# The upper halves of the first three units' values, issued by ScalarE instead of SyncE

## The chip, the cores and the metric

The kernel runs on one core of a Trainium2 chip. A core has TensorE (PE: matmuls, and the loads of their weights, PEld), VectorE (DVE), ScalarE (ACT), GpSimd (POOL) and SyncE (SP), each with its own instruction stream, and 16 DMA engines. SyncE here only issues transfers; ScalarE computes and can issue transfers too. The metric is the time of one execution on the device in microseconds, lower is better.

## The reference

Chunked attention with memory rows feeds a gated feed-forward layer with spatial mixing. Batch 4, 8 heads, 768 positions, head size 64; chunks of 32 positions.

```python
for c in range(nc):                       # 24 chunks
    l_start, r_end = max(0, c_start - 16), min(S, c_end + 8)
    k_full = concat([mem_k, k[:, :, l_start:r_end]])      # 8 memory rows first
    v_full = concat([mem_v, v[:, :, l_start:r_end]])
    a = softmax(scale * q_c @ k_full.T)
    out[:, :, c_start:c_end] = a @ v_full
x = out as (batch, seq, 512)
h = relu(x @ w_in)                        # 512 x 1024
u, v = h[..., :512], h[..., 512:]
v_n = (v - mean) / sqrt(var + 1e-6)
v_s = einsum('ts,bsd->btd', w_spatial, v_n) + b_spatial
y = (u * v_s) @ w_out
```

## The kernel before

The attention is cut into 24 units of four chunks (six units for each batch). For a unit `i` the steps are: ScalarE copies its keys into a padded tile (`prep`, L375, `kmain`); TensorE multiplies 64 small tiles of queries and keys into `sx` (L388, `sx<-kmain,q`, "scores"); VectorE takes the row maximum and subtracts it (L441, L445); ScalarE's exponential (L450) makes `p`; VectorE sums and inverts (L455, L456, L458, `den` and `rec`); TensorE transposes `p` (L472, `pt`), ScalarE copies it (L475, `pT`); TensorE multiplies with the values (L388, `sx<-vmain,pT`, "product with values"); VectorE normalises (L424, `xs`); TensorE transposes `xs` (L487, `xt`); ScalarE's cast (L492) and VectorE's subtraction (L496) split the result into a high and a low part of `x`. `sx` has one buffer: the product of unit i - 1 shares a buffer with the scores of unit i, and the next pair waits until both have been read.

The feed-forward product runs in three matmuls for each piece (L525 to L527, `f`: high by high, low by high, high by low). Its weights `w_in` come in eight pieces of 512 columns by 128 rows, four for the second half of the columns (needed first) and four for the first half. Each piece is loaded into one of four `big` buffers and prepared in steps on three engines: ScalarE scales it twice (L825, L830), VectorE does a shift pair (L834, L835), GpSimd adds (L840), ScalarE casts to the high part (L854), and VectorE or GpSimd subtracts for the low part (L858, `win_l`).

Values: `load_v(i)` fetches a unit's values into its third of `vmain`. The lower half of the partitions (r = 0) takes the even heads and the upper half (r = 1) the odd ones, each in two transfers, of 32 rows (128 KB) and of 24 rows (96 KB); the eight rows between hold the memory values. All of these stand on SyncE, in the order in which the code lists them with the queries, keys and weights (`line` ties each to the one ahead).

No engine's order is written out by hand. Every step is an `op` with an engine, an estimated time, what it reads and writes and a rank; `Plan.order` runs a list schedule with these estimates, and all instructions are emitted in the order of its start times. A transfer's estimated end is its size times `drag` by a rate, added to the end of the one ahead. So a change of one load's engine, of its `drag` or of what it stands behind (`after`) moves rows on all engines. On the chip each engine works through its rows strictly in that order. Transfers of all engines take one of eight completion counters in turn, and one is issued only when the transfer eight before it has landed; `held_by` adds a limit on the bytes under way.

## Time and profile before

| | |
|---|---|
| median of 3 runs | 380.65 us (380.58 to 384.18) |
| the profiled execution | 378.39 us, span 376.2 us |
| TensorE busy | 355.6 us (95%) |
| VectorE busy | 275.0 us (73%) |
| ScalarE busy | 188.8 us (50%) |
| GpSimd busy | 139.8 us (37%) |
| share of TensorE in the chain that ended last | 91% |

Times in the rows are microseconds from the start of the span. A row of the timeline has its start, its duration, the engine, the line, the operation, the tile written and the tile read, the shapes, and in brackets how long the engine was idle before it and what ended that. SPq and ACTq are the issues of transfers by SyncE and ScalarE. A row of the waits has total time, number of times and the longest. A row of stretches has the stretch, its length, busy time (and number of instructions) of PE, PEld, DVE, ACT and POOL, the clock granted to TensorE (1.00 is full), the mean busy share of the DMA engines and their GB/s.

### The profile page before, as it was taken

The numbers are of one execution on the slowest core, as the hardware profiler recorded it, in microseconds if no ns is written. First come the engines' busy times: TensorE is split into PE (matmuls) and PEld (weight loads), VectorE is DVE, ScalarE is ACT, GpSimd is POOL, SyncE is SP. The second block draws the span as 40 slices with busy tenths as digits, with TensorE's granted clock in tenths as the row PEclk, the third lists the DMA queues.
The fourth block names the chain that finished last, engine by engine and source line by source line (L and its number), as shares of the span: only waits on it lengthen the run. The fifth ranks groups of instructions, "written<-read, shape, count | busy, mean of one in ns | idle before, by whom it ended". The sixth has DMA issues, their size and how long they took to land.

```text
span 376.2 us, 11734 instructions
## 1 busy us (share of the span) xinstructions
PE 355.6 (95%) x4964; PEld 327.8 (87%) x4964; DVE 275.0 (73%) x470; ACT 188.8 (50%) x336; POOL 139.8 (37%) x143
## 2 busy tenths in 40 slices
PE   1569899999999999999999999999999999999996
PEld 1357698898988988989889899999999999999996
DVE  3887875757767667775498589787858795896694
ACT  3757544554654456354473366327533742553371
POOL 5444652383484088510033195251026002203410
PEclk9969999999999999999999999999999999999999
DMA  8998888888786783865832649204720582140014
GB/s 230 290 233 228 186 250 232 230 234 250 218 237 192 251 232 92 264 212 181 233 142 92 216 142 319 101 0 167 250 89 0 170 257 80 61 144 8 2 44 167
DMA packets 47368, 65.12 MB, mean 173 GB/s; under 512 B 4434, under 2 KB 38866, under 8 KB 47316
## 3 DMA queue, kind: packets, MB, share of 16 engines
q1 hardware_dynamic: 46900, 64.25, 56.4%
q8 instruction: 39, 0.64, 0.7%
q10 hardware_dynamic: 416, 0.13, 0.1%
q14 instruction: 13, 0.11, 0.1%
HBM read 45.49 MB, written 18.87 MB: 171 GB/s over the span
## 4 chain that ended last, share of the span: by engine, by line
PE 91%; DVE 4%; ACT 2%; DMA 1%; issue 1%; SPq 0%; ACTq 0%; DVEq 0%
PE y L686 22%; PE f L686 17%; PE f L525 13%; PE f L526 12%; PE f L527 12%; PE sx L388 10%; PE xt L487 3%; PE pt L472 3%; DMA k<-in_k_dram 1%; DVE st L835 1%; DVE st L834 1%; DVE mx L441 1%; DVE p L445 0%; PE y L680 0%; PE f L680 0%
## 5 line engine op out<-in xcount | busy, mean ns | idle before, releaser
L742 POOL TENSOR_TENSOR ug<-st,ug 128x384 f32<-128x384 f32 x24 | 33.1, 1392 | 97.7 <-DVE st L734 97.7
L686 PE MATMUL y<-wsp,op 128*128 128x384 f32 x288 | 52.6, 336 | 0.0
L686 PEld LDWEIGHTS y<-wsp,op 128*128 128x128 f32 x288 | 50.1, 188 | 0.0
L525 PE MATMUL f<-x,win_h 128*128 128x384 f32 x128 | 46.3, 362 | 0.0
L527 PE MATMUL f<-x,win_h 128*128 128x384 f32 x128 | 43.1, 337 | 0.0
L526 PE MATMUL f<-x,win_l 128*128 128x384 f32 x128 | 43.0, 336 | 0.0
L525 PE MATMUL f<-win_h,x 128*128 128x512 f32 x96 | 41.7, 435 | 0.0
L686 PE MATMUL f<-wsp,op 128*128 128x384 f32 x216 | 40.1, 336 | 0.0
L526 PE MATMUL f<-win_h,x 128*128 128x512 f32 x96 | 38.6, 402 | 1.5 <-DVE x L496 1.5
L664 DVE TENSOR_TENSOR op<-sm,op 128x768 fp32r<-128x768 f32 x32 | 33.4, 1050 | 7.2 <-ACT op L661 6.6
L527 PE MATMUL f<-win_l,x 128*128 128x512 f32 x96 | 38.4, 400 | 0.0
L686 PEld LDWEIGHTS f<-wsp,op 128*128 128x128 f32 x216 | 37.6, 188 | 0.0
L686 PE MATMUL y<-wout,op 128*128 128x256 f32 x288 | 35.7, 280 | 0.0
L424 DVE TENSOR_TENSOR xs<-sx,rec 128x512 f32<-128x512 f32 x24 | 16.5, 689 | 25.8 <-PE sx L388 25.6
L686 PEld LDWEIGHTS y<-wout,op 128*128 128x128 f32 x288 | 34.8, 188 | 0.1
L661 ACT CAST op<-sm 128x768 fp32r<-128x768 f32 x32 | 26.3, 838 | 15.5 <-DVE sm L647 7.7
L571 POOL TENSOR_TENSOR rstd<-ve,mhalf 128x1 f32<-128x1 f32 x24 | 14.6, 610 | 52.2 <-DVE ve L567 51.8
L388 PEld LDWEIGHTS sx<-kmain,q 64*32 64x32 f32 x1536 | 17.5, 110 | 17.1 <-POOL vmain L370 9.5
L388 PE MATMUL sx<-kmain,q 64*32 64x64 f32 x1536 | 21.5, 235 | 10.6 <-ACT kmain L375 8.4
L596 ACT ACTIVATE uo<-f 128x384 f32<-128x384 f32 x32 | 15.6, 491 | 24.5 <-PE f L527 23.0
L370 POOL COPY vmain<-memv 8x1024 f32<-8x1024 f32 x22 | 23.5, 1075 | 10.2 <-PE sx L388 8.5
L686 PE MATMUL f<-wout,op 128*128 128x256 f32 x216 | 27.1, 280 | 0.0
(92 smaller groups left out, 732.8 us busy)
## 6 DMA issues: line engine op xcount, KB each, us to landing
vmain<-in_v_dram SPq DMA_DIRECT2D x48, 128.0 KB
vn_far<-st SPq DMA_DIRECT2D x24, 256.0 KB
u_far<-uo SPq DMA_DIRECT2D x32, 192.0 KB
vr<-vn_far SPq DMA_DIRECT2D x8, 768.0 KB
ug<-u_far SPq DMA_DIRECT2D x16, 384.0 KB
q<-in_q_dram SPq DMA_DIRECT2D x11, 512.0 KB
out_dram<-ot SPq DMA_DIRECT2D x36, 128.0 KB
vmain<-in_v_dram SPq DMA_DIRECT2D x47, 96.0 KB
```

Source lines behind the costliest of these rows:

```text
L370: {"DVE": nc.vector, "POOL": nc.gpsimd}[eng].tensor_copy(to, of)
L388: nc.tensor.matmul(o, w_, m, start=True, stop=True, skip_group_check=True)
L424: nc.vector.tensor_tensor(xs.rearrange("p t r d -> p r t d"), t_["sx", i][:, :, 1], rec.rearrange("p t r -> p r t").unsqueeze(3).broadcast ...
L525: nc.tensor.matmul(o, lh, rh, start=(j == 0), stop=False)
L526: nc.tensor.matmul(o, ll, rh, start=False, stop=False)
L527: nc.tensor.matmul(o, lh, rl, start=False, stop=(j == len(pairs) - 1))
L571: nc.gpsimd.tensor_tensor(a, t_["ve", i], mhalf, op=ALU.pow)
L596: op("ACT", act(HT), lambda: nc.scalar.activation(alloc("uo", i, [P, HT], F32), t_["f", n], AF.Relu), r=[("f", n)], w=[("uo", i)], rank=rank)
L661: nc.scalar.copy(half(0), of())
L664: nc.vector.tensor_tensor(half(1), of(), half(0).bitcast(F32), op=ALU.subtract)
L686: nc.tensor.matmul(o, x, y, start=first and m == 1 and not (seed and bank != "x"), stop=m == 3 * chunks, skip_group_check=True)
L742: nc.gpsimd.tensor_tensor(g, t_[st(x)], g, op=ALU.mult)
```

## The change

For units 0, 1 and 2, the two transfers of the upper half of the partitions no longer stand in SyncE's line. They are issued by ScalarE, behind the start of its copy of the same unit's keys (`prep`). The estimate's factor `drag` is 1.2 instead of 1.5 for all transfers of these units' values. From unit 3 on, `load_v` is as it was.

```diff
-    def load_v(i, seq=True, second="SP"):
+    def load_v(i, heads=(0, 1), eng="SP", drag=1.5, after=None):
+
         b, c0 = i // UB, (i % UB) * UC
         n = UC
-        for r in range(2):
+        for r in heads:
...
-                load(dst, src_, w=[("vm", i, r, s)], rank=10.0 * i, slow=1.2, us=0.38, seq=seq, drag=1.5,
-                     eng=second if r else "SP")
+                load(dst, src_, w=[("vm", i, r, s)], rank=10.0 * i, slow=1.2, us=0.38, seq=eng == "SP", drag=drag, eng=eng, after=after)
...
         if i < NU:
             prep(i, rank)
+            if i < 3:
+                load_v(i, (1,), "ACT", 1.2, len(plan.ops) - 1)
         burst(i, rank, split)
...
-    load_v(0)
+    load_v(0, (0,), drag=1.2)
...
-    load_v(1)
+    load_v(1, (0,), drag=1.2)
...
-    load_v(2)
+    load_v(2, (0,), drag=1.2)
```

`load` takes the new argument `after` and hands it to `op`, for loads that are not in a line. Below L505 the changed kernel's line numbers are higher by two.

VectorE's rows from the second shift pair to the first `xs`, before. The numbers tell buffers apart: `st_264`, `st_281`, `st_289` and `st_307` are the first four pieces of `w_in`, `p_287` belongs to unit 1, and `xs_364` is the first normalised result.

```order
L858 TENSOR_TENSOR win_l_110<-st_264,win_h_109 128x512
L834 TENSOR_SCALAR st_289<-st_289 128x512
L835 SCALAR_TENSOR_TENSOR st_289<-big_170,st_289 128x512
L834 TENSOR_SCALAR st_307<-st_307 128x512
L835 SCALAR_TENSOR_TENSOR st_307<-big_172,st_307 128x512
L858 TENSOR_TENSOR win_l_110<-st_281,win_h_109 128x512
L424 TENSOR_TENSOR xs_364<-sx_230,rec_269 128x2x4x64
L455 TENSOR_REDUCE den_366<-p_287 128x8
```

The same place in the changed kernel, where the fourth piece is `st_306` and the first `xs` is `xs_372`:

```order
L860 TENSOR_TENSOR win_l_110<-st_264,win_h_109 128x512
L836 TENSOR_SCALAR st_289<-st_289 128x512
L837 SCALAR_TENSOR_TENSOR st_289<-big_170,st_289 128x512
L860 TENSOR_TENSOR win_l_110<-st_281,win_h_109 128x512
L455 TENSOR_REDUCE den_321<-p_287 128x8
L456 TENSOR_TENSOR den_321<-den_321,eps_104 128x8
L458 RECIPROCAL rec_324<-den_321 128x8
L860 TENSOR_TENSOR win_l_110<-st_289,win_h_109 128x512
L836 TENSOR_SCALAR st_306<-st_306 128x512
L837 SCALAR_TENSOR_TENSOR st_306<-big_172,st_306 128x512
L424 TENSOR_TENSOR xs_372<-sx_230,rec_269 128x2x4x64
```

The sum and reciprocal of unit 1 and one more subtraction for `win_l` have moved ahead of the first `xs`.

ScalarE's rows at the same place of the program, from the last scaling of the fourth piece to the cast of unit 0's result, before:

```order
L830 ACTIVATE big_172<-big_172 128x512
L450 ACTIVATE p_287<-p_287 128x512
L854 CAST win_h_109<-st_281 128x512
L475 COPY pT_362<-pt_318 128x512
L854 CAST win_h_109<-st_289 128x512
L492 CAST x_380<-xt_371 128x4x128
L375 COPY kmain0_144<-k_224 128x20x32
L854 CAST win_h_109<-st_307 128x512
L375 COPY kmain1_145<-k_224 128x20x32
```

And in the changed kernel:

```order
L257 DMA vmain_143<-in_v_dram 32x4x256
L856 CAST win_h_109<-st_281 128x512
L257 DMA vmain_143<-in_v_dram 24x4x256
L450 ACTIVATE p_287<-p_287 128x512
L856 CAST win_h_109<-st_289 128x512
L475 COPY pT_367<-pt_326 128x512
L375 COPY kmain0_144<-k_224 128x20x32
L257 DMA vmain_143<-in_v_dram 32x4x256
L257 DMA vmain_143<-in_v_dram 24x4x256
L375 COPY kmain1_145<-k_224 128x20x32
L856 CAST win_h_109<-st_306 128x512
L492 CAST x_423<-xt_413 128x4x128
```

The exponential of unit 1 stands behind the cast of the second piece, the copies of the keys of units 2 and 3 stand ahead of the fourth piece's cast and of the cast of unit 0's result, and four of the six new issues are seen here (the first two stand between the copies of the keys of units 0 and 1). A little later the scaling of the sixth piece (L827, `big_311`) stands ahead of the exponential of unit 2.

TensorE, from the warming matmuls (L540, L542 in the changed kernel) to the first matmul of the dense stream, before:

```order
L540 MATMUL f_299<-win_h_109 128x512 x4
L472 MATMUL pt_318<-ident_102,p_287 128x128 x4
L388 MATMUL sx_230<-vmain_143,pT_279 32x64 x32
L487 MATMUL xt_371<-ident_102,xs_364 128x128 x4
L388 MATMUL sx_389<-kmain0_144,q_182 32x64 x32
L525 MATMUL f_427<-win_h_109,x_380 128x512
```

And in the changed kernel:

```order
L542 MATMUL f_299<-win_h_109 128x512 x4
L472 MATMUL pt_326<-ident_102,p_287 128x128 x4
L388 MATMUL sx_230<-vmain_143,pT_279 32x64 x32
L388 MATMUL sx_377<-kmain0_144,q_178 32x64 x32
L487 MATMUL xt_413<-ident_102,xs_372 128x128 x4
L527 MATMUL f_434<-win_h_109,x_423 128x512
```

The scores of unit 2 and the transposes of the first `xs` have changed places; the same work stands ahead of the dense stream. Behind it, the next two products with values come after nine and twelve `f` matmuls, in place of twelve and twelve. From the second half of TensorE's rows on, both kernels have the same order.

## The prediction

> **What bounds the kernel now.** The page comes first. The profiled execution took 378.39 us, 376.2 of them span; TensorE is busy 95% of it, and only the first slices of its row are not 9.

> ```profile
> PE   1569899999999999999999999999999999999996
> PEclk9969999999999999999999999999999999999999
> ```

> The stretches say where the idle time is.

> ```profile
> 0.00:24.58 24.58, 9.26 (x272) 6.69 (x272) 16.93 (x30) 13.71 (x24) 12.09 (x17) 0.95 0.97 255
> 24.58:44.00 19.42, 17.41 (x317) 13.31 (x313) 16.32 (x32) 11.26 (x20) 10.54 (x10) 0.88 0.91 221
> 44.00:365.00 321.00, 320.97 (x4316) 300.00 (x4315) 236.14 (x399) 160.87 (x287) 117.14 (x116) 1.00 0.53 165
> 365.00:376.20 11.20, 7.97 (x69) 7.76 (x67) 5.61 (x12) 2.98 (x8) 0.00 (x0) 1.00 0.41 142
> ```

> The first number after the stretch is its length, the second TensorE's busy time. From 44 to 365 us TensorE is idle for 0.03 us, so nothing that is made earlier there can be felt. What can move is when the dense stream of `f` matmuls begins (24.58 us), what it loses before 44 us (2.0 us idle), and the clock meanwhile. The last 11 us keep their order of instructions. The kernel is bound by TensorE, and a change in the loads is worth only what it does to the first 44 us.

> So next the waits of TensorE, and its row of events up to the first dense matmul.

> ```profile
> PE sx L388 <- ACT kmain L375: 8.4, 2, 7.1
> PE f L540 <- ACT win_h L854: 2.9, 1, 2.9
> PE xt L487 <- DVE xs L424: 1.9, 1, 1.9
> PE f L526 <- DVE x L496: 1.5, 1, 1.5
> ...
> 18.66 0.98 PE L388 MATMUL sx<-vmain,pT 64*32 64x64 f32 x64
> 21.51 0.66 PE L487 MATMUL xt<-ident,xs 128*128 128x128 f32 x4 [1.87 <-DVE xs L424]
> 23.47 1.19 PE L388 MATMUL sx<-kmain,q 64*32 64x64 f32 x64 [1.30 <-ACT kmain L375]
> 24.58 0.80 PE L525 MATMUL f<-win_h,x 128*128 128x512 f32 x1
> ```

> No wait names the values (`vmain` as a DMA). The first product with values, at 18.66, stands behind the transposes of unit 1's `p`. Were the values late for it? The issue rows of SyncE answer, since a transfer is issued only when the one eight before it has landed.

> ```profile
> 17.37 0.97 SPq L257 DMA_DIRECT2D big<-in_moe_w_in_dram  x1
> 21.24 0.30 SPq L257 DMA_DIRECT2D vmain<-in_v_dram  x1
> 27.60 0.32 SPq L257 DMA_DIRECT2D vmain<-in_v_dram  x1
> ```

> The first row waits for the last of unit 0's values, which are there by 17.37, 1.3 us before 18.66. The second waits for the keys of units 2 and 3 (landed 21.24), the third for the sixth piece of `w_in` (landed by 27.60). The values are not what TensorE waits for; between 18.66 and 21.51 it waits for VectorE's `xs`. VectorE in these microseconds:

> ```profile
> 17.53 0.69 DVE L835 SCALAR_TENSOR_TENSOR st<-big,st 128x512 uint32<-128x512 uint32 x1
> 18.14 0.42 DVE L834 TENSOR_SCALAR st<-st 128x512 uint32<-128x512 uint32 x1
> 18.59 1.66 DVE L835 SCALAR_TENSOR_TENSOR st<-big,st 128x512 uint32<-128x512 uint32 x1
> 20.18 0.68 DVE L858 TENSOR_TENSOR win_l<-st,win_h 128x512 fp32r<-128x512 f32 x1
> 20.78 0.68 DVE L424 TENSOR_TENSOR xs<-sx,rec 128x512 f32<-128x512 f32 x1
> 21.38 0.67 DVE L455 TENSOR_REDUCE den<-p 128x8 f32<-128x512 f32 x1
> 22.08 0.17 DVE L456 TENSOR_TENSOR den<-den,eps 128x8 f32<-128x8 f32 x1
> 22.28 0.20 DVE L458 RECIPROCAL rec<-den 128x8 f32<-128x8 f32 x1
> ```

> VectorE never rests here, so the order of its rows decides when `xs` comes.

> **The change part by part.** *Two DMA issues removed from SyncE and two added to ScalarE, three times.* ScalarE's issue of two transfers is in the trace once:

> ```profile
> 1.27 0.92 ACTq L257 DMA_DIRECT2D memv<-in_mem_v_dram  x2
> ```

> So each pair takes 0.92 us of ScalarE's sequencer. Unit 0's pair runs beside the keys copy that it stands behind (0.73, quoted below), and in the wait for the second keys that follows; unit 1's stand behind a weight scaling and a cast, with only the exponential of unit 1 behind them; unit 2's run beside the next keys copy. Cost 0, hidden by those copies; without that cover 0.92 us each, 2.8 in all. The waits that these issues carry are for transfers that came eight earlier, which had landed in the rows above; I price them at 0, and their upper end is the late-landing rival below. What SyncE saves is its own time, and it was waiting for landings, not for its issues: 0.

> *The order on VectorE ahead of the first `xs`.* This is the term that decides. Up to the end of the second shift pair (17.53 + 0.69 = 18.22) both orders are the same. Then stood a shift pair, one `win_l` and `xs`. Now stand one `win_l`, unit 1's `den`, `add` and reciprocal, another `win_l`, the shift pair, and `xs`. The second `win_l` needs GpSimd's sum and ScalarE's cast:

> ```profile
> 18.35 1.35 POOL L840 TENSOR_TENSOR st<-st,big 128x512 uint32<-128x512 uint32 x1 [1.14 <-DVE st L835]
> 20.39 1.61 POOL L840 TENSOR_TENSOR st<-st,big 128x512 uint32<-128x512 uint32 x1 [0.69 <-ACT pT L475]
> ...
> 17.45 0.63 ACT L854 CAST win_h<-st 128x512 fp32r<-128x512 f32 x1
> 22.69 0.73 ACT L375 COPY kmain<-k 128x640 f32<-128x640 f32 x1
> ```

> 18.22 + 0.68 + (0.67 + 0.17 + 0.20) = 19.94; the sum on GpSimd ends at 19.70 and the cast at 20.35, so `win_l` runs 20.4 to 21.1; the shift pair, now alone (in the old order its second half took 1.66 beside GpSimd, otherwise 0.69), adds 0.42 + 0.69 and ends at 22.2. `xs` starts at 22.2 in place of 20.78: **1.4 us later**.

> *From `xs` to the dense stream.* Now the scores of unit 2 stand ahead of the transposes. `xs` ends at 22.9; the keys landed at 21.24 and are copied by 22.0; scores 22.9 to 24.0 (1.11 from 23.47 to 24.58 in the old rows); transposes 0.66 at the full clock, about 1.1 at half, to 25.1; cast 0.6 (as the cast above) and `x` low 0.68 (as the subtraction of `win_l`) to 26.4. The first `f` matmul can go at 25.7, the second at 26.4; a stream in step with that begins at 26.0 against 24.58: **+1.4**, or +1.0 where the transposes run at 0.66.

> *The clock.* These stretches are the profiler's own clock steps; the number behind the engines is the granted clock.

> ```profile
> 18.95:22.36 3.41, 1.35 (x68) 0.95 (x51) 3.34 (x6) 1.26 (x3) 2.37 (x2) 1.00 1.08 272
> 22.36:25.77 3.41, 2.30 (x67) 1.94 (x68) 3.02 (x7) 3.35 (x6) 0.00 (x0) 0.50 0.88 206
> 25.77:29.19 3.42, 3.42 (x10) 2.65 (x9) 2.33 (x5) 0.63 (x1) 1.29 (x1) 0.50 1.00 232
> 36.01:39.43 3.42, 1.91 (x9) 1.16 (x8) 3.39 (x5) 2.50 (x5) 2.33 (x3) 1.00 0.70 207
> ```

> A stretch with 1.35 busy (40%) was followed by half clock, one with 2.30 (67%) did not end it, one with 3.42 did, and one with 1.91 (56%) did not bring it back. Dense work at half clock was 29.19 - 24.58 = 4.6 us, a loss of 2.3; now 29.19 - 26.0 = 3.2, a loss of 1.6: **-0.7**. [...]

> *The second product with values, near 32 us.* Nine `f` matmuls at 0.42 each end near 29.6, then unit 2's transposes (0.66), a product (0.98) and three `f` (0.7) reach 31.8 or so. The next product needs VectorE's second `xs`. On ScalarE the exponential of unit 2 now stands behind the scaling of the sixth `w_in` piece: 27.6 + 0.63 + 0.63 = 28.9, each taken as the cast of the same 512 columns; `den` with its two small steps 1.04 to 30.0; a shift pair 1.11 to 31.1; `xs` 0.68 to 31.8. That would just do. But GpSimd's `win_l` subtraction falls on the shift pair, as here in the old order:

> ```profile
> 35.74 1.33 POOL L858 TENSOR_TENSOR win_l<-st,win_h 128x512 fp32r<-128x512 f32 x1 [0.73 <-ACT win_h L854]
> 35.84 1.52 DVE L834 TENSOR_SCALAR st<-st 128x512 uint32<-128x512 uint32 x1
> ```

> 1.52 in place of 0.42 is **+1.1** of new idle time (0 if they miss each other). The old 1.5 us wait for `x` low comes again behind it, at the third transposes: no difference.

> The sum: 1.4 - 0.7 + 1.1 = +1.8 us. On the profiled execution that is 380.2. Its 378.39 lies 2.3 us below the median of the runs, 380.65, and under their lowest, about what one and a half clock steps are worth; the forecast for the median is 380.65 + 1.8 = **382.4 us**. Both ends of the unknowns: transposes at 0.66 and no collision give 1.0 - 0.7 = +0.3, so 381.0; a lost cover of 0.92 on top gives 383.4.

> **The rivals.** *The old order's end (same time):* collision missed, values moved for nothing, 380.0 to 381.2. For it speaks that GpSimd and VectorE meet only by tenths of a microsecond. That the values arrive no earlier, so that the change does not do what it says, ends here too, because they were not waited for.

> *Faster:* with fewer transfers queued ahead on SyncE, the last `w_in` pieces are issued sooner, and GpSimd's and VectorE's preparation runs ahead, so that neither the collision nor the old 1.5 us wait recurs: 1.4 - 0.7 - 1.5 = -0.8, 379.8. Against it: VectorE, not a landing, bounds `xs`, and the gain begins only behind 30 us.

> *Slower, the sixth `w_in` piece late:* ScalarE's exponential of unit 2 stands behind that piece's scaling. Unit 2's upper values, 224 KB, now come on ScalarE's own queue while that piece is still on SyncE's.

> ```profile
> vmain<-in_v_dram SPq DMA_DIRECT2D x48, 128.0 KB
> vmain<-in_v_dram SPq DMA_DIRECT2D x47, 96.0 KB
> ```

> At the 221 GB/s of the second stretch 229,000 bytes take 1.0 us. If they go first, the piece lands at 28.6 and exponential, `den`, `xs` and product follow 1.0 us later: +2.8, 383.4; if unit 1's do so too, 384.5. It decides from a landing later than 27.6. [...] No run here shows two queues loaded at once, so it has a chance, not the lead.

> *Slower, the clock:* a new stretch under about half busy brings another step at half clock, up to 1.7 us: 384.1.

> **How the numbers follow.** The forecast (381.2 to 383.0) has 0.48, the same-time rival 0.22, the faster one 0.08, the late piece 0.14, the clock 0.08. The range takes in all but the outer halves of the last three: 379.6 to 385.0. 1% is 3.8 us, about what a measurement of this kernel can tell from no change: under 376.8 needs an earlier dense stream, which the order of VectorE excludes unless all is misread, 0.03; over 384.5 takes a part of the late piece and of the clock, and an unseen wait in the reordered middle, 0.11; within, 0.86.

> **What would show it.** Right: `xs` first at about 22.2, the first `f` matmul at 25.5 to 26.4, a wait of TensorE for L424 near 32 us, no idle time from 45 to 365. Wrong: `xs` before 21.5 (the shift pair or casts earlier than I place them), or the exponential of unit 2 after 29.5 with ScalarE waiting for `big` (the late piece), or TensorE idle in the middle.

## The result: 384.88 us, a ratio of 1.008 to before

| | before | changed |
|---|---|---|
| median | 380.74 us (20 runs, 379.10 to 386.05) | 384.88 us (20 runs, 379.54 to 389.53) |
| ratio | | 1.008 (1.0054 to 1.0106) |
| profiled execution | 378.39 us, span 376.2 | 389.53 us, span 387.5 |

Ratios leave out runs that lie far above the shortest of their kernel and medians do not; the profiled run of the changed kernel is its longest, so two more profiles of it (387.75 and 383.68 us) and one more of before (380.38 us) stand beside it below. By the medians the change costs 4.1 us.

The slices of the changed kernel's page: TensorE's row has two dips more, and the row of the granted clock falls at another place. This trace has no clock record ahead of 32.59 us, and the views show full clock where there is none; what the spacing of the matmuls says of that time comes below.

```profile
PE   1548799899999999999999999999999999999996
PEclk9999699999999999999999999999999999999999
```

The stretches, as those of before were cut, with the border at the first `f` matmul of this run:

```profile
0.00:28.77 28.77, 9.92 (x273) 7.11 (x273) 16.61 (x30) 14.06 (x24) 12.13 (x17) 1.00 0.96 245
28.77:45.00 16.23, 12.33 (x222) 9.32 (x223) 10.83 (x22) 8.88 (x16) 6.17 (x6) 0.83 0.76 174
45.00:100.00 55.00, 52.99 (x1117) 45.41 (x1117) 37.94 (x74) 26.55 (x47) 26.35 (x31) 0.99 0.74 213
```

The dense stream begins at 28.77 in place of 24.58. From there to 45 us TensorE is idle for 3.9 us, from 45 to 100 for 2.0 us, where before had 0.03 us idle up to 365.

Now the rows of the steps, VectorE first, then ScalarE, then TensorE. Here and below the rows that matter are picked; those between them are left out.

```profile
22.45 0.69 DVE L424 TENSOR_TENSOR xs<-sx,rec 128x512 f32<-128x512 f32 x1
...
16.49 0.32 ACTq L257 DMA_DIRECT2D vmain<-in_v_dram  x1
17.23 0.30 ACTq L257 DMA_DIRECT2D vmain<-in_v_dram  x1
...
23.32 0.72 ACT L375 COPY kmain<-k 128x640 f32<-128x640 f32 x1 [1.57 <-DMA k<-in_k_dram]
24.53 2.42 ACTq L257 DMA_DIRECT2D vmain<-in_v_dram  x2
26.99 0.72 ACT L375 COPY kmain<-k 128x640 f32<-128x640 f32 x1 [2.95 <-DMA vmain<-in_v_dram]
28.14 0.58 ACT L492 CAST x<-xt 128x512 fp32r<-128x512 f32 x1
...
28.77 0.80 PE L527 MATMUL f<-win_h,x 128*128 128x512 f32 x1 [2.45 <-ACT x L492]
35.17 0.96 PE L388 MATMUL sx<-vmain,pT 64*32 64x64 f32 x64
36.06 0.66 PE L487 MATMUL xt<-ident,xs 128*128 128x128 f32 x4
36.65 0.78 PE L388 MATMUL sx<-kmain,q 64*32 64x64 f32 x54
39.76 0.45 PE L388 MATMUL sx<-kmain,q 64*32 64x64 f32 x10 [2.34 <-issue]
41.72 1.08 PE L487 MATMUL xt<-ident,xs 128*128 128x128 f32 x4 [1.51 <-DVE x L496]
56.92 0.34 PE L529 MATMUL f<-x,win_h 128*128 128x384 f32 x1 [0.77 <-issue]
75.09 0.33 PE L388 MATMUL sx<-vmain,pT 64*32 64x64 f32 x12 [1.24 <-issue]
```

Three things are to be seen. `xs` starts at 22.45, as forecast (22.2). On ScalarE the two issues of unit 2 (24.53) hold the engine for 2.42 us; the next keys copy names the values as what ended its wait, and the cast that the dense stream needs stands behind it. By the count of eight, they wait for unit 1's pair, issued at 16.49 and 17.23; in the trace they use the same two completion counters as that pair, whose last steps come at 24.51 and 26.62, each 0.02 us ahead of one of the two issues (24.53 and 26.64). And TensorE pauses 2.34 us in the middle of unit 3's 64 score products, after the 54th, waiting for nothing that the profile shows; two smaller pauses follow. Then the granted clock:

```profile
36.00:39.41 3.41, 1.42 (x71) 1.03 (x58) 0.91 (x3) 3.08 (x6) 1.80 (x4) 1.00 0.96 259
39.41:46.24 6.83, 4.97 (x23) 3.98 (x24) 5.29 (x10) 1.11 (x2) 0.94 (x2) 0.50 0.40 90
```

The stretch that holds the pause has 1.42 us of work, and half clock follows for 6.83 us.

### The profile page after: what moved, and what is told of

Read it like the earlier page. It is cut to its first block, busy times and chain, and to the rows that moved or that the text cites. A ratio compares the mean times of both kernels' runs of the same rounds, so it can differ in the third digit from the quotient of the medians.

```text
span 387.5 us, 11740 instructions
## 1 busy us (share of the span) xinstructions
PE 358.8 (93%) x4964; PEld 329.3 (85%) x4964; DVE 275.6 (71%) x470; ACT 187.5 (48%) x336; POOL 139.8 (36%) x143
## 4 chain that ended last, share of the span: by engine, by line
PE 90%; DMA 6%; issue 1%; DVE 1%; ACT 1%; ACTq 0%
PE y L688 22%; PE f L688 16%; PE f L527 13%; PE f L528 12%; PE f L529 12%; PE sx L388 9%; PE xt L487 3%; PE pt L472 3%; DMA big<-in_moe_w_in_dram 2%; DMA vmain<-in_v_dram 2%; DMA memv<-in_mem_v_dram 1%; PE y L682 0%; PE f L682 0%; DVE x L496 0%; ACTq L257 0%
## 5 line engine op out<-in xcount | busy, mean ns | idle before, releaser
L424 DVE TENSOR_TENSOR xs<-sx,rec 128x512 f32<-128x512 f32 x24 | 16.5, 689 | 29.9 <-PE sx L388 29.8
L388 PEld LDWEIGHTS sx<-kmain,q 64*32 64x32 f32 x1536 | 17.6, 111 | 21.2 <-POOL vmain L370 9.3
L388 PE MATMUL sx<-kmain,q 64*32 64x64 f32 x1536 | 21.9, 235 | 14.5 <-ACT kmain L375 10.2
L663 ACT CAST op<-sm 128x768 fp32r<-128x768 f32 x32 | 26.3, 838 | 17.1 <-DVE sm L649 10.4
L573 POOL TENSOR_TENSOR rstd<-ve,mhalf 128x1 f32<-128x1 f32 x24 | 13.5, 564 | 55.6 <-DVE ve L569 55.2
L370 POOL COPY vmain<-memv 8x1024 f32<-8x1024 f32 x22 | 23.6, 1078 | 12.6 <-PE sx L388 10.9
## 6 DMA issues: line engine op xcount, KB each, us to landing
vmain<-in_v_dram SPq DMA_DIRECT2D x45, 128.0 KB
out_dram<-ot SPq DMA_DIRECT2D x36, 128.0 KB
```

The costliest lines, as they stand in the source:

```text
L370: {"DVE": nc.vector, "POOL": nc.gpsimd}[eng].tensor_copy(to, of)
L388: nc.tensor.matmul(o, w_, m, start=True, stop=True, skip_group_check=True)
L424: nc.vector.tensor_tensor(xs.rearrange("p t r d -> p r t d"), t_["sx", i][:, :, 1], rec.rearrange("p t r -> p r t").unsqueeze(3).broadcast ...
L573: nc.gpsimd.tensor_tensor(a, t_["ve", i], mhalf, op=ALU.pow)
L663: nc.scalar.copy(half(0), of())
```

## Looking again: what recurs and what is chance

Before and the changed kernel were run again, unchanged, each for another profile.

> The kernel before, unchanged, for a second profile, since its first one lay 2.3 us under the median of its runs. Theory F with chance (the pauses of TensorE at the ends of blocks of 256 instructions differ from run to run of one program): a run at 380 to 384 us shows a pause of 1 to 3 us at the product near 34 us, as 54 + 10, or at a later block end, where the first profile had 0.28. Rival (the old order never pauses long, only the clock differs): the pause stays under 0.5 and the dense stream begins at 24.3 to 25.0 again.

> The changed kernel, unchanged, for a second profile, since its first one was the longest of its 20 runs. What is the program's own and recurs: ScalarE's third pair of issues taking over 2 us, the second keys copy behind it, the dense stream at 27.5 to 29. What is chance: the size of the pause at 54 + 10 in unit 3's scores (2.3 before; 0 to 3.5 now) and those at about 57 and 75 us. A typical run is 383 to 386 us. Rival (all of the first profile is the program's own): 2.3 again within 0.5, and about 388 us.

> The same program once more, for the same question: the dense stream at 27.5 to 29 again, and a pause at 54 + 10 that differs from the two others by more than 0.5 us if it is chance.

Before again, 380.38 us, TensorE's rows:

```profile
24.43 0.80 PE L525 MATMUL f<-win_h,x 128*128 128x512 f32 x1
33.22 0.33 PE L388 MATMUL sx<-vmain,pT 64*32 64x64 f32 x10 [1.11 <-issue]
61.54 0.50 PE L526 MATMUL f<-win_h,x 128*128 128x512 f32 x1 [0.56 <-issue]
66.92 0.35 PE L388 MATMUL sx<-vmain,pT 64*32 64x64 f32 x17 [0.70 <-issue]
93.28 0.27 PE L388 MATMUL sx<-vmain,pT 64*32 64x64 f32 x2 [1.09 <-issue]
```

The changed kernel's second profile (387.75 us), TensorE's rows, the stretch that the pause fills, and the one at half clock:

```profile
26.94 0.79 PE L527 MATMUL f<-win_h,x 128*128 128x512 f32 x1 [1.89 <-ACT x L492]
40.05 0.45 PE L388 MATMUL sx<-kmain,q 64*32 64x64 f32 x10 [3.46 <-issue]
```

```profile
36.60:40.02 3.42, 0.00 (x0) 0.00 (x0) 0.00 (x0) 1.60 (x3) 1.50 (x3) 1.00 1.04 270
40.02:46.84 6.82, 5.29 (x24) 4.11 (x25) 5.60 (x10) 1.12 (x2) 0.80 (x1) 0.50 0.15 51
```

And its third (383.68 us), the nearest to the median: ScalarE's and TensorE's rows, and two stretches:

```profile
22.63 2.35 ACTq L257 DMA_DIRECT2D vmain<-in_v_dram  x2
25.02 0.72 ACT L375 COPY kmain<-k 128x640 f32<-128x640 f32 x1 [2.44 <-DMA vmain<-in_v_dram]
26.80 0.80 PE L527 MATMUL f<-win_h,x 128*128 128x512 f32 x1 [1.58 <-ACT x L492]
38.27 0.33 PE L388 MATMUL sx<-kmain,q 64*32 64x64 f32 x10 [1.80 <-issue]
```

```profile
36.02:39.43 3.41, 0.78 (x52) 0.45 (x31) 0.76 (x2) 1.99 (x4) 1.86 (x3) 1.00 0.84 233
39.43:42.84 3.41, 2.73 (x9) 2.38 (x10) 2.81 (x5) 1.12 (x2) 0.00 (x0) 0.50 0.11 31
```

ScalarE's wait at these issues (2.95, 3.44 and 2.44 us of idle time ahead of the second keys copy), the late start and the split after 54 products recur in all three; the length of the pause does not (2.34, 3.46, 1.80). The start came earlier than I expected here (26.8 and 26.9, not 27.5 to 29). Before has a pause too, at 54 + 10 of the product near 33 us, 0.28 and 1.11 long. In its first profile, with the wait for `x` low that follows:

```profile
33.75 0.33 PE L388 MATMUL sx<-vmain,pT 64*32 64x64 f32 x10 [0.28 <-issue]
39.33 0.50 PE L526 MATMUL f<-win_h,x 128*128 128x512 f32 x1 [1.51 <-DVE x L496]
```

These rows make up the difference in span, as terms against the first profile of before. At half clock the `f` matmuls come 0.43 us apart, at full clock 0.23; from these two numbers I take, as an estimate, half of TensorE's work in a stretch at half clock as lost. At the head of the stream half clock lasts from the first `f` until the products come closer: before to 29.19, that is 2.3 us lost. The ends in the changed kernel's columns are read from this spacing.

| us | changed, 1st | 2nd | 3rd | before again |
|---|---|---|---|---|
| first `f`, against 24.58 | +4.2 | +2.4 | +2.2 | -0.2 |
| half clock at the head, to 32.5, 33.2, 32.6, 26.4, against 2.3 | -0.4 | +0.8 | +0.6 | -1.3 |
| pause at 54 + 10, against 0.28 | +2.1 | +3.2 | +1.5 | +0.8 |
| half clock behind the pause | +2.5 | +2.6 | +1.4 | 0 |
| later pauses (the first with 0.5 of ScalarE's `st` at 250 us, the second 0.48 at 57 and 0.65 at 75 us) | +2.5 | +1.1 | 0 | +2.4 |
| sum | 10.9 | 10.1 | 5.7 | 1.7 |
| span, against 376.2 | 11.3 | 9.5 | 5.5 | 2.0 |

## Whose fault: ScalarE's issues or the new order of rows

Theory A says the new order of rows that the planner made, theory B says the issues on ScalarE. In the first of these experiments the changed order is kept on all engines and SyncE issues the six transfers.

```diff
+        e = {"SP": nc.sync, "ACT": nc.scalar, "POOL": nc.gpsimd}[by or eng]
...
+            load(..., eng=eng, after=after, by="SP" if i in (0, 1, 2) else None)
```

> The changed kernel's rows on TensorE, VectorE and GpSimd, and ScalarE's without its six new issues; those six are issued by SyncE. Theory A (my prediction's: the new order on VectorE costs the time) expects the changed kernel's time, 1.008 of the kernel before, and no gain against it: first xs at 22.4, dense f stream from about 28. Theory B (ScalarE is held by its issues, and transfers on its queue are slow, so the keys of units 2 and 3 and the cast of unit 0's result come late) expects the keys to land near 21.2, the cast at 25.5 to 26.3 with no wait for a transfer ahead of it, the dense stream at 26.0 to 26.7 and a time of 1.002 to 1.005.

```profile
21.82 1.35 ACT L375 COPY kmain<-k 128x640 f32<-128x640 f32 x2
25.75 0.79 PE L527 MATMUL f<-win_h,x 128*128 128x512 f32 x1 [0.67 <-ACT x L492]
39.53 0.33 PE L388 MATMUL sx<-kmain,q 64*32 64x64 f32 x10 [3.66 <-issue]
```

385.58 us, ratio 1.0128 (1.0072 to 1.0183). Both keys copies run without a wait and the dense stream begins at 25.75, inside the 25.7 to 26.4 of the prediction: so the rest of the delay in the changed kernel comes with ScalarE's issues. But the total did not fall; this run's pause is 3.66.

Next, the same edit for unit 2 alone (`i in (2,)`), and for unit 0 alone (`i in (0,)`).

> As the changed kernel, but unit 2's upper pair is issued by SyncE; units 0 and 1 stay with ScalarE. Theory A: 1.008, as the changed kernel. Theory B, part one (unit 2's issues hold ScalarE for 2.4 us ahead of the cast): the second keys copy follows the first without a wait, the cast comes near 26.4 (when the transposes end), the dense stream at about 27 in place of 28.8, and the time is 1.003 to 1.006. The keys still land near 23.3.

> As the changed kernel, but unit 0's upper pair is issued by SyncE. Theory B, part two (unit 0's pair on ScalarE's queue lands only at 13.2, and the issue of the keys of units 2 and 3 waits for that counter): those keys are issued near 10.8 and land near 21.3, the scores of unit 2 start at about 23.1 in place of 24.1, while unit 2's issues may still hold ScalarE ahead of the cast, to about 26 or 27; time 1.005 to 1.008. If the keys land near 23.3 again, the counter is not the cause. Theory A: 1.008.

```profile
22.39 1.35 ACT L375 COPY kmain<-k 128x640 f32<-128x640 f32 x2 [1.07 <-DMA k<-in_k_dram]
38.64 0.45 PE L388 MATMUL sx<-kmain,q 64*32 64x64 f32 x10 [3.17 <-issue]
```

That is unit 2's pair on SyncE: 386.40 us, ratio 1.0137 (1.0077 to 1.0196). The wait between the keys copies is gone (the first `f` starts at 26.07), the pause stays. With unit 0's pair on SyncE (ratio 1.0054, 0.9998 to 1.0111; median 387.77) it is there again:

```profile
23.02 3.15 ACTq L257 DMA_DIRECT2D vmain<-in_v_dram  x2
26.21 0.73 ACT L375 COPY kmain<-k 128x640 f32<-128x640 f32 x1 [2.53 <-DMA vmain<-in_v_dram]
```

So it is unit 2's issue that waits, and unit 0's has no part in it. Last, the order of before with ScalarE issuing the six transfers at their old places (`by="ACT" if r and i < 3 else None` in the code of before).

> The kernel before with its own rows and estimates; the six transfers are issued by ScalarE at the places that the old schedule gave them. Theory A (the order on VectorE): the time of the kernel before, 1.000. Theory B (issuing by ScalarE and its queue): slower, with ScalarE waiting for a landing at the pair of unit 2, which stands ahead of the copy of pT and the cast of unit 0's result; dense stream 1 to 3 us later than 24.6, time 1.003 to 1.008.

```profile
22.76 0.59 ACT L475 COPY pT<-pt 128x512 f32<-128x512 f32 x1 [3.20 <-DMA k<-in_k_dram]
26.14 0.80 PE L525 MATMUL f<-win_h,x 128*128 128x512 f32 x1
35.18 0.32 PE L388 MATMUL sx<-vmain,pT 64*32 64x64 f32 x10 [0.75 <-issue]
```

381.77 us, ratio 1.0019 (0.9977 to 1.006). ScalarE's issues delay the dense stream here too (26.14 against 24.58), and the time stays. Old order 1.000 and 1.002, new order 1.013 and 1.008: this speaks for theory A, that the order costs it, though not by the way that the prediction priced. It is not settled by these runs: the interval of the old order with ScalarE's issues reaches 1.006 and that of the changed kernel begins at 1.0054, and the new order does not always pause. In the profile with unit 0's pair on SyncE (384.73 us) unit 3's scores go through with a gap of 0.11 us.

## What the pause is

A burst of 64 matmuls (x64) in the trace is 128 instructions, a weight load and a matmul each. Theory F: the pause is the end of a block of TensorE's instructions that had not been brought yet. The page's list of DMA queues has, under the kind instruction, one with 39 packets:

```profile
q8 instruction: 39, 0.64, 0.7%
```

39 packets with 0.64 MB are 16 KB each. TensorE has 10,009 instructions in this trace, 256.6 for each of the 39 packets; that the queue is TensorE's and a packet a block of 256 instructions is an estimate from these two numbers. With 39 or 40 packets in each of fourteen profiles there are some 550 ends of such blocks, and 25 pauses over 0.6 us (counted below), of 3.66 us at most: at most of the ends TensorE does not pause that long. To test the place, 59 tiny products were put at TensorE's head, 236 instructions (each is two weight loads and two matmuls in the trace).

```diff
+            if i == 0:
+                for _ in range(59):
+                    mm(sx[0:CH, 0, 0, 0], ident[0:D, 0:CH], ident[0:D, 0:D])
```

> The changed kernel with 59 tiny extra products of 32x64 on the identity, 236 instructions, at the head of TensorE's program, where it waits for the keys anyway; they write where unit 0's scores are put later, so the result is the same. Every later instruction of TensorE stands 236 places further on, nothing else moves. Theory F (the new order loses its time in TensorE's instruction stream: the 54 + 10 split of unit 3's scores near 37 us is the end of a block of 256 instructions that had not been brought yet, and the half clock at 39 to 46 us follows from that pause): the split leaves unit 3's scores and goes to the product at 35 us, as 4 + 60; the next block's end falls between unit 3's scores and the third transposes, where TensorE waits 1.5 us for x low anyway, so a pause there costs 0 to 1.5. No half clock behind 39 us, median 381 to 383.5, ratio to before 1.000 to 1.006, about 1 to 3 us under the change. Rival D (the time is lost because the dense stream begins 2 to 4 us later, whatever the stream of instructions does): ratio 1.008 to 1.013 as the change and its variants had, with or without a split. If the split stays at 54 + 10, it is no block's end, and theory F falls.

```profile
1.41 12.69 PE L388 MATMUL sx<-ident 64*32 64x64 f32 x117 [1.41 <-POOL ident masks.py:199]
40.63 0.86 PE L388 MATMUL sx<-kmain,q 64*32 64x64 f32 x64
44.61 1.09 PE L490 MATMUL xt<-ident,xs 128*128 128x128 f32 x4 [3.12 <-DVE p L448]
76.32 0.94 PE L388 MATMUL sx<-vmain,pT 64*32 64x64 f32 x62
79.36 0.27 PE L388 MATMUL sx<-vmain,pT 64*32 64x64 f32 x2 [2.10 <-issue]
```

As a test of the time it failed: 395.85 us, ratio 1.0311 (1.0234 to 1.0388), because the extra products, all into one place, took 12.69 us and held up the first scores. As a test of the place it is clear. Unit 3's scores run whole: ten pairs later than 54 is their very end, 64. The pause is not gone, it stands behind them: the third transposes, which waited 1.51 us for `x` low in the changed kernel, wait 3.12 here, and half clock follows (43.44 to 50.27). The profile puts this wait down to a subtraction of VectorE that ended at 44.14. The product ahead of unit 3's scores, which I had expected to be split 4 + 60, runs whole at 39.16: not every block's end makes a pause. The product that was split 52 + 12 at 75.09 is now split 62 + 2: 256 - 236 = 20 instructions, ten pairs, later. In the changed kernel's trace the splits at 39.76 and 75.09 lie 1279 instructions apart (matmuls, weight loads and the sequencer's own), five blocks of 256 less one. Counted so over all fourteen profiles, there are 25 pauses of TensorE over 0.6 us with no releaser, and each stands 192 or 193 places past a multiple of 256. The pause is a block's end.

The traces hold the fetches too. TensorE has 10,009 instructions and the queue 39 packets of 16 KB; with the extra products there are 10,245 and 40. After each of the 25 pauses TensorE goes on 1.2 to 1.9 us after the end of one of these packets, and so it does behind the wait of 3.12 (packet's end 43.02, next matmul 44.61). For the block behind 54 + 10 the packet itself takes 1.0 to 1.4 us. What differs is when it starts:

| us | packet starts, after the block ahead begins | pause |
|---|---|---|
| order of before: first, again, with ScalarE's issues | 0.9, 1.7, 0.9 | 0.28, 1.11, 0.75 |
| changed kernel: 1st, 2nd, 3rd | 3.1, 4.3, 2.9 | 2.34, 3.46, 1.80 |
| its order, on SyncE: all six, unit 2's pair, unit 0's pair | 5.5, 4.6, 0.7 | 3.66, 3.17, 0.11 |

TensorE goes through the block ahead in 3.2 us in the order of before and in 3.3 to 3.5 us in the changed kernel, so it is not TensorE that is faster here: the fetch starts later.

Why is the block late? Theory L: its fetch stands behind loads issued just ahead of it. Five loads were cut to a quarter of their bytes, which leaves out three quarters of unit 3's values and of the third pair's queries.

```diff
+        thin = w[0][:2] in (("vm", 3), ("q", 2))
...
+            if thin:
+                to, of = to[:, 0:1], <the first quarter of the source>
...
```

> The changed kernel where the loads that are issued between 27.9 and 33 us bring a quarter of their bytes: the four transfers of unit 3's values and the one of the third pair's queries, 0.96 MB to 0.24 MB; the number of transfers, their order and their waits stay. Three quarters of those values and queries are left out, so units 3, 4 and 5 compute with old ones. Theory L (the block of TensorE's instructions that unit 3's scores pause for comes late because its fetch stands behind these loads): the pause shrinks from 2.3 to 3.7 us to under 0.8, the split stays at 54 + 10, no half clock behind 39 us, median 381 to 383.5, ratio 1.000 to 1.006. Rival S (TensorE asks for the block late itself, because it goes through it in one burst): the pause stays at 2 us or more, ratio 1.007 to 1.014.

> The changed kernel with a quarter of the bytes in five loads, once more (it leaves out three quarters of unit 3's values and of the third pair's queries). Its first profile had no pause, but it was the shortest of its 12 runs, whose median is 385.7. If the fetch of TensorE's instructions stands behind those loads (theory L), there is no pause over 0.8 us at 54 + 10 again, and the lost time is in the late dense stream and the clock. If not, a run at 384 to 388 us shows a pause of 1.5 to 3.5 us there.

385.67 us, ratio 1.0058 (1.0003 to 1.0113). The first profile, of its shortest run (379.21), has unit 3's scores whole, and it is as fast as a short run of before although its first `f` starts at 26.69; the second (388.15) has this:

```profile
38.48 0.33 PE L397 MATMUL sx<-kmain,q 64*32 64x64 f32 x10 [2.79 <-issue]
```

Theory L falls for these five loads: with a quarter of their bytes the pause is 0 or 2.79, differing between runs of one program, and the packet starts 0.8 or 3.4 us after the block ahead begins. What makes a fetch start late stays open; other loads were not taken away.

## Two other plans

With the factor 1.2 for the first three units' values in the planner and nothing else of the change, and with the change made for unit 0 alone:

```diff
-                load(..., drag=1.5, ...)
+                load(..., drag=1.2 if i < 3 else 1.5, ...)
```

> Before with one part of the change alone: the planner is told that the first three units' values weigh 1.2 in place of 1.5 in the queue of loads; all of them stay on SyncE, four a unit. VectorE's rows up to the first xs are those of before; TensorE's differ in two places (unit 1's transposes of p behind the first product with values, unit 4's scores a few rows later). By theory F the block ends fall where they fell in before (in the product at 34 us, 54 + 10), so a pause under 1 us: ratio 0.997 to 1.004. Rival (the planner's number itself costs the time): 1.008 or more.

```diff
-            if i < 3:
+            if i < 1:
                 load_v(i, (1,), "ACT", 1.2, len(plan.ops) - 1)
...
-    load_v(1, (0,), drag=1.2)
+    load_v(1, drag=1.2)
...
-    load_v(2, (0,), drag=1.2)
+    load_v(2, drag=1.2)
```

> The change for unit 0 alone, planned anew: its upper rows by ScalarE behind its keys, units 1 and 2 whole on SyncE, weight 1.2 for the three. TensorE's order up to 24 us is that of before again (transposes of xs ahead of unit 2's scores), with one weight subtraction less ahead of xs on VectorE. Term of the prediction: xs 0.7 us sooner than in the change, dense stream at 24 to 25 us. Theory F: the block that ends in the second product holds two sets of transposes, unit 2's scores and that product, as dense as before, so a pause of 0.3 to 1 us; ratio 0.998 to 1.005. Rival D says the same from another reason (dense stream as in before); a ratio over 1.008 speaks against both and for ScalarE's queue.

382.54 us, ratio 1.0049 (1.0007 to 1.0091), and 385.84 us, ratio 1.0073 (1.002 to 1.0126). Their pauses in the second product, one row each:

```profile
35.36 0.33 PE L388 MATMUL sx<-vmain,pT 64*32 64x64 f32 x10 [2.41 <-issue]
```

```profile
35.73 0.45 PE L388 MATMUL sx<-vmain,pT 64*32 64x64 f32 x11 [2.69 <-issue]
```

I had expected under 1 us for both, wrongly: an old place of the block's end does not keep the pause short. Here, too, the packet starts late (2.7 and 3.1 us after the block ahead begins). No version was faster than before.

## Why the prediction was right in its total and wrong in its places

Forecast 382.4 (379.6 to 385.0), measured 384.88: inside the range by 0.1 us, 2.5 us above the middle. Where +1.8 was forecast, the medians differ by 4.1. That the change stays within 1% holds for the ratio, 1.008, and not for the median, which lies over the 384.5 that the prediction named. That the total fell into the range is in part luck: the collision and the gain of clock did not come, and a wait priced at 0 and a pause that is in no part of the prediction took their place. (Of the sums, the lost cover gives 382.4 + 0.92 = 383.3, not 383.4.)

- *VectorE's order, `xs` at 22.2:* right. 22.45, 22.04 and 22.22 in the three profiles. The term +1.4 for the start of the dense stream is what remains when ScalarE's issues are taken away (25.75, +1.2).
- *"The waits that these issues carry ... I price them at 0":* the step that failed. I took the transfers eight earlier as landed, as in the rows of before, but with the change they are, by the count of eight, the pair that ScalarE itself had issued at 16.49 and 17.23, and it needed until 24.5 and beyond. The issues took 2.42, 1.59 and 2.35 us in the three profiles, with ScalarE idle for 2.95, 3.44 and 2.44, and the first `f` went at 26.80 to 28.77, not 25.7 to 26.4: 1.0 to 3.0 later than the 25.75 without these issues. In the 28.77 the keys, too, came late (1.57 waited at 23.32). The cover that I named, the keys copies, was itself behind the wait.
- *The clock, -0.7:* mis-sized. The late start took -0.4 at best; in two of three profiles the head of the stream lost 0.6 to 0.8 more than before. In the first profile the `f` matmuls come 0.43 us apart up to 32.3 while the clock column says 1.00; its clock records begin only at 32.59 (33.19 and 32.60 in the others), so here the rows' spacing decides.
- *GpSimd beside VectorE at the second product, +1.1:* did not happen. At 35.17 TensorE takes up the product, and at 36.06 the transposes, without a wait for L424.
- *"The old 1.5 us wait for x low comes again ... no difference":* the wait is the same 1.51; what is new is the pause at the block's end ahead of it. In the first and second profiles the pause alone empties a stretch (1.42 and 0.00 us of work in 3.41), and the wait for `x` low comes only in the next one; in the third a pause of 1.80 and the first part of that wait share a stretch (0.78). Each time the clock halves. In before, where the pause was 0.28, the stretch with the wait alone had 1.91 and kept it. The place of the pause among its neighbours does not decide it: in the two other plans, where `f` matmuls follow the pause, the stretch in which the pause of 2.69 began had 1.70 us of work and half clock followed, and that of 2.41, divided over two stretches (2.15 and 2.08), cost no clock. This is the rival "the clock", priced at 1.7; it cost 1.4 to 2.6 in the changed kernel's profiles, and its trigger, the block's end, was in no part of the prediction though the row 33.75 of before shows it (0.28).
- *No idle time from 45 to 365:* wrong in two of three profiles, by later block ends.
- *The late sixth piece and the faster case* played no part in the changed kernel's total.

That the parts add up is shown by the table, and that the pause is TensorE waiting for its next block of instructions by the places and the packets. That the new order makes this fetch late is not shown: eight profiles with that order have pauses of 1.80 to 3.66 in six and of 0.11 or none in two, three with the order of before have 0.28 to 1.11, and 2.41 and 2.69 came up in two other orders.

## What to carry to other kernels

Unit 2's two transfers, issued by ScalarE, brought the wait for their completion counters into its stream (2.42 us at 24.53, and 2.95 us idle ahead of the next keys copy): before moving a transfer to an engine that computes, find the one whose landing it waits for in the *changed* order and price that wait on the next instruction behind. Count TensorE's instructions to the block ends: bursts of tiny products go through 256 of them in about 3.3 us here, and where the fetch started 3.1 us after the block ahead began, the pause was 2.34 us and 6.83 us at half clock followed. No run here found an order that avoids it. Where runs of one program differ by 10 us, one profile is not the program: take two or three before pricing a difference of 1%.

## What the hardware showed that I had not expected

```profile
q1 hardware_dynamic: 1193, 1.79, 89.4%
q10 hardware_dynamic: 246, 0.22, 16.6%
```

- 117 tiny matmuls into one place of PSUM took 12.69 us, 108 ns each; 64 of the same shape into many places take 0.86 us, 13 ns each. The 117 also share one weight; which of the two costs the time was not tested.
- In all fourteen profiles, a stretch of 3.41 us on record at full clock was followed by half clock where TensorE had 1.72 us of work in it or less, twelve times ahead of the last microseconds (at most 1.72, in the run with unit 2's pair on SyncE), and by full clock where it had 1.81 or more (the least in the run with unit 0's pair on SyncE).
